# An attention and feed-forward kernel on one core: the last group's second layer as seven block products, and the first value loads on another queue

## The chip, the cores and the metric

The kernel runs on one core of a Trainium2 chip. A core has TensorE (PE in the profile, with PEld for its weight loads), VectorE (DVE), ScalarE (ACT), GpSimd (POOL) and SyncE (SP), each with its own instruction stream, which it works off in order; they wait for one another by semaphores only. DMAs are issued by SP or ACT and run on 16 DMA engines that all queues share. The metric is the device time of one execution, in microseconds; the figure for a kernel is the median of several runs.

## The reference

Two stages, for q, k, v of shape (4, 8, 768, 64) in float32:

```python
k_sum, v_sum = k.reshape(B, H, 24, 32, D).max(axis=3), v.reshape(B, H, 24, 32, D).mean(axis=3)
scores_l = where(|i - j| < 16, scale * q @ k.T, -1e9)
scores_s = scale * q @ k_sum.T + log(32)
a = softmax(concat([scores_l, scores_s], -1))
x = (a @ concat([v, v_sum])) -> (B, 768, 512)            # heads side by side
xn = (x - mean(x)) / sqrt(var(x) + 1e-6) * g_ln
out = x + maximum(xn @ w_ch1, 0) @ w_ch2                  # 512 -> 2048 -> 512
```

## The kernel before, in words

The 3072 rows are 24 tiles of 128 rows (T), and 12 groups of two tiles (g). Attention goes by half tiles (t = 0 to 47, four heads each). The first eight (t < 8, the `early_...` steps) work in float32 while the weights arrive; the others split every operand into a high and a low float16 part and sum three products (hh times high, hh times low, hl times high). The weights are fetched as 32 blocks (`fetch_w`, tile `raw`), decoded by DVE and ACT (`dec_w`, tile `wf`), scaled and split into two float16 parts (`conv_w`, tile `wp`).

The feed-forward layer of groups 0 to 5 is plain (`g1`, `g2`). Groups 6 to 11 (`SG = 6`) use seven block products in place of eight for the first layer (`split1`, `split2`, `sp1`; the sums of weight blocks are built by `combine`, tiles `wd`), and a plain second layer: `sp2`, two output tiles, each a sum of 8 times three products of 512 columns for either half q of the hidden units. For the very last tile and q = 1 that sum is cut into two halves of 256 columns (tile `last`). `kout` scales the result, a DVE instruction adds it to x (`scalar_tensor_tensor`, x<-a,wsc,x in the profile), and SP writes it out.

Steps only record their instructions. `Plan` then orders them: a list scheduler with a table of durations (`cost`, `ISSUE`, `LAND`, `RATE`), waits with some slack (`slack`), and random starts; the order that does best in a rehearsal with random DMA delays is issued. `LOADS` fixes the head of SP's queue (`in_front`), `BESIDE` says which of those loads ACT issues. Where the scheduler expects PE to stand idle before the weights are there, it fills in transposes (`spare`); `warm` puts 36 transposes at the start.

In the start, SP loads keys (k), queries (qw), the block matrix (blk), values (vw, two halves per tile) and weights; ACT issues the second half of the values of the first six tiles. PE works on score products (s), transposes of probabilities (pp), block means of values (v), outputs (o), transposes of normalised rows (tx) and then the first layer (h). In the profile nearly all instructions carry the line of the issuing helper, L437, so groups are told apart by tile names.

Of the kernel before, what the change touches and what calls it, by code (L numbers as in the profile page):

```python
# [50 lines left out]
SG = 6  # L51
# [11 lines left out]
LOADS = [("fetch_k0", 0), ("fetch_k0", 1), ("fetch_q", 0), ("gain",), ("fetch_blocks",), ("fetch_k0", 2), ("fetch_k0", 3)]  # L63
LOADS += [("fetch_v0", c) for c in range(7)] + [("fetch_tail", 0), ("fetch_q", 1), ("fetch_tail", 1), ("fetch_tail", 2)]
BESIDE = [("fetch_v0", c, 1) for c in range(6)]
# [33 lines left out]
def in_front(stage, engine):  # L99


    key = (stage[0], *stage[1][:1])
    return LOADS.index(key) if engine == "sync" and key in LOADS else None


class Plan:
# [6 lines left out]
    SETUP, TICK, SWITCH, FIRST = 1100, 10240 / 3, 93, 3500  # L113
    ISSUE = dict(transp=1550, lnT=1250, batch_vput=760, load_q=500)
    LAND = dict(fetch_v0=2050, fetch_k0=1950, fetch_q=2000, fetch_w=1750, fetch_tail=2000, gain=2000)
# [92 lines left out]
    def cost(self, engine, op, a, k, ins, outs):  # L208
# [3 lines left out]
        if op[:3] == "dma":  # L212
            x = (outs + ins)[0]
            return self.ISSUE.get(self.names[self.stage][0], 380 + 70 * (engine == "scalar")), x.ap[0][1] * free(x) * mybir.dt.size(x.dtype) / (200.0 if "transpose" in op else 360.0)
# [51 lines left out]
    def slack(self, x, y):  # L266

        name, a = self.names[x.stage]
        if x.engine == "tensor":
            if name in ("g1", "g2"):  # L270
                return SLACK2 * (a[0] >= 24)
            if name in ("sp1", "sp2"):
                return SLACK2 if name == "sp2" or self.names[y.stage][0] != "sp1" else SLACKP
            return SLACK * (name in ("qk", "pv", "batch_s"))
# [3 lines left out]
        late |= name in ("g1", "g2") and a[0] >= 24 or name in ("sp1", "sp2", "split1", "split2")  # L278
# [163 lines left out]
def body(ctx: ExitStack, tc, qt, qa, qe, kt, ks, va, vb, vs, g_ln, w1, w2, blocks, out):  # L442
# [654 lines left out]

    def operand(g, *names):
# [42 lines left out]
    def sp1(g, q):  # L1141
# [52 lines left out]
        keep("21", z)  # L1194
        product(x, "s4", plain(1, 1), last=True)
        keep("12", x)

# [32 lines left out]
    @pl.step  # L1230
    def gain():
        nc.sync.dma_start(gcol[:, 0], g_ln.rearrange("(c p) -> p c", p=P))
        nc.scalar.activation(gcol[:, 1], gcol[:, 0], AF.Copy, scale=SQ)

# [55 lines left out]

    warm()
# [37 lines left out]
    for t in range(8, 2 * TT + 1):  # L1329
# [82 lines left out]
```

## Time and profile before

| | |
|---|---|
| three runs | 615.63, 615.76, 616.48 us (median 615.76) |
| profiled execution | 614.82 us, of which span 613.0 us |
| mean granted TensorE clock | 0.997 (0.91 and 0.75 in the stretches 10 to 15 and 15 to 20 us) |
| HBM traffic | 66.27 MB read, 6.29 MB written |

The span runs from the first to the last instruction of the profiled execution; 1.8 us of its time lie around it. Busy shares are means over stages that have different limits, so the stretches in the rows below are cut where the stage changes: the first layer's first product starts at 48.46 us, the last matmul but six ends near 609.24 us. The duration of one matmul in the profile overlaps its neighbours; the pace of matmuls is read from the pieces of the chain of waits, where "x6" stands beside the time of six.

### The profile page before, as it was taken

How to read it: one execution, taken by the hardware profiler on the slowest of the kernel's cores; microseconds unless marked ns; L12 is line 12 of the kernel's file. 1: busy time of each engine (PE TensorE's matmuls, PEld its weight loads, DVE VectorE, ACT ScalarE, POOL GpSimd, SP SyncE). 2: the span in 40 equal slices, each digit the busy share in tenths (PEclk: the TensorE clock that was granted, in tenths of full speed). 3: DMA queues.
4: the chain of work that ended last, by engine and by line, in shares of the span. 5: the costliest groups of instructions: out<-in, count | busy, mean ns of one | idle time of the engine just before them, and what ended most of it. 6: DMA issues, size and time to landing. Idle time of an engine off the chain costs nothing.

```text
span 613.0 us, 15408 instructions
## 1 busy us (share of the span) xinstructions
PE 596.3 (97%) x5528; PEld 434.0 (71%) x5528; DVE 493.4 (80%) x1260; ACT 429.0 (70%) x1072; POOL 249.0 (41%) x473
## 2 busy tenths in 40 slices
PE   6998899999999999999999999999999999999997
PEld 5586777765677587776866876877777778766675
DVE  3899999999899899999798988889788974633232
ACT  3797798878999977799777857788686575331120
POOL 5122212124675575767664452645445333200000
PEclk9999999999999999999999999999999999999999
DMA  8991388636988977679966757569668461220000
GB/s 250 341 350 31 115 263 279 195 86 138 237 224 203 204 194 181 161 173 220 208 161 150 172 121 152 143 154 198 138 155 180 94 126 45 44 61 18 18 18 35
DMA packets 136237, 95.62 MB, mean 156 GB/s; under 512 B 94561, under 2 KB 118625, under 8 KB 136161
## 3 DMA queue, kind: packets, MB, share of 16 engines
q1 hardware_dynamic: 134528, 93.86, 60.6%
q8 instruction: 43, 0.70, 0.5%
q10 hardware_dynamic: 1632, 0.79, 0.5%
q14 instruction: 34, 0.27, 0.1%
HBM read 66.27 MB, written 6.29 MB: 118 GB/s over the span
## 4 chain that ended last, share of the span: by engine, by line
PE 75%; DVE 13%; DMA 5%; ACT 3%; POOL 2%; issue 1%; SPq 0%; ACTq 0%; POOLq 0%
PE a L437 34%; PE h L437 12%; PE qx L437 10%; PE qz L437 5%; PE s L437 4%; PE o L437 4%; PE qy L437 3%; DVE wf L437 2%; DMA vw<-in_va 1%; DVE raw L437 1%; DVE hl L437 1%; DVE wp L437 1%; PE v L437 1%; DMA ksg<-in_kt 1%; DVE p L437 1%
## 5 line engine op out<-in xcount | busy, mean ns | idle before, releaser
L437 PE MATMUL a<-wp,hh 128*128 128x512 f16 (+1 forms) x768 | 226.6, 377 | 0.0
L437 PEld LDWEIGHTS <-wp 128*128 128x128 f16 x2016 | 163.2, 98 | 25.0 <-issue 2.3
L437 PE MATMUL a<-wp,hl 128*128 128x512 f16 x384 | 144.8, 377 | 0.0
L437 PE MATMUL h<-xs,wp 128*128 128x256 f16 x1152 | 134.1, 273 | 2.2 <-DMA xs<-x 1.0
L437 PEld LDWEIGHTS <-hh 128*128 128x128 f16 x784 | 73.3, 98 | 65.3 <-issue 0.4
L437 POOL TENSOR_TENSOR p<-p,p 128x512 f16<-128x512 f32 x72 | 71.9, 1004 | 35.3 <-ACT p L437 24.5
L437 ACT ACTIVATE p<-p,mn,sv 128x184 f32<-128x184 f32 x144 | 76.1, 530 | 9.1 <-POOL mn L437 8.5
L437 PEld LDWEIGHTS <-hl 128*128 128x128 f16 x392 | 38.3, 98 | 44.6
L437 DVE SCALAR_TENSOR_TENSOR x<-a,wsc,x 128x512 f32<-128x512 f32 (+1 forms) x48 | 35.3, 736 | 22.4 <-PE a L437 22.1
L437 POOL COPY ksg<-ksum 128x48 f32<-128x48 f32 x72 | 29.3, 412 | 52.1 <-DMA ksg<-in_kt 44.8
L437 POOL TENSOR_TENSOR x<-x,rc 128x256 f32<-128x256 f32 x36 | 30.5, 847 | 42.5 <-DVE x L437 31.7
L437 POOL TENSOR_SCALAR mn<-mn,sv 128x2 f32<-128x2 f32 x72 | 31.1, 434 | 40.4 <-DVE mn L437 37.6
L437 DVE CUSTOM_DVE_ANT_0 p<-s,mask 128x184 f32<-128x184 f32 x144 | 42.7, 337 | 3.6 <-PE s L437 3.6
L437 PE MATMUL qx<-xs,wp 128*128 128x128 f16 x576 | 38.4, 219 | 0.0
L437 PEld LDWEIGHTS <-wd 128*128 128x128 f16 x576 | 33.8, 98 | 3.1
L437 DVE SCALAR_TENSOR_TENSOR kl<-ksg,sv,kh 128x368 f16<-128x368 f32 x48 | 34.2, 721 | 1.5 <-ACT kh L437 1.2
L437 ACT ACTIVATE kh<-ksg,sv 128x368 f16<-128x368 f32 x48 | 28.5, 594 | 9.4 <-PE s L437 3.4
L437 DVE SCALAR_TENSOR_TENSOR hl<-h,hh 128x512 f16<-128x512 f32 x48 | 32.3, 678 | 2.0 <-ACT hh L437 1.8
L437 ACT CAST p<-p 128x512 f16<-128x512 f32 x72 | 33.3, 505 | 0.2
L437 ACT ACTIVATE v<-vst,sv 128x512 f16<-128x512 f32 x36 | 25.7, 716 | 9.2 <-PE o L437 7.8
L437 DVE SCALAR_TENSOR_TENSOR v<-vst,sv,v 128x512 f16<-128x512 f32 x36 | 30.2, 838 | 1.3 <-ACT v L437 1.1
L437 ACT ACTIVATE hh<-h 128x512 f16<-128x512 f32 x48 | 28.0, 584 | 4.4 <-PE h L437 4.3
(209 smaller groups left out, 1217.0 us busy)
## 6 DMA issues: line engine op xcount, KB each, us to landing
raw<-in_w SPq DMA_DIRECT2D x32, 512.0 KB
ksg<-in_kt SPq DMA_DIRECT2D x72, 184.0 KB
out_x<-x SPq DMA_DIRECT2D x23, 256.0 KB
qw<-in_qt SPq DMA_DIRECT2D x36, 128.0 KB
vst<-in_va SPq DMA_DIRECT2D x36, 128.0 KB
qs<-in_qt SPq DMA_DIRECT2D x36, 128.0 KB
vst<-in_vb SPq DMA_DIRECT2D x80, 32.0 KB
bst<-in_ks SPq DMA_DIRECT2D x12, 192.0 KB
```

The lines of the kernel that those rows point to most:

```text
L437: getattr(getattr(nc, self.ops[i].engine), op)(*a, **k)
```

## The change

Three things are edited. The group g = 11 (`SH = 11`) gets a second layer of seven block products of 256 columns (`sq2`): `sp1` then also builds sums of the rectified hidden blocks (s1 to s4), and `combine2` builds sums of blocks of the second weight matrix (tiles y, we) on POOL, DVE and ACT, in the places of tiles that attention no longer needs (`WE`). The six value halves move from ACT's queue to SP's (`BESIDE = []`), and a step `table` puts a dummy exponential at the head of ACT. The planner's table of the first loads' durations is changed and `LOADS` is reordered.

```diff
-SG = 6
+SG, SH = 6, 11
...
-BESIDE = [("fetch_v0", c, 1) for c in range(6)]
+LOADS += [("fetch_v0", c) for c in range(7)] + [("fetch_tail", 0), ("fetch_w", 0), ("fetch_q", 1), ("fetch_tail", 1)]
+LOADS += [("fetch_w", 1), ("fetch_tail", 2)]
+BESIDE = []
...
-    SETUP, TICK, SWITCH, FIRST = 1100, 10240 / 3, 93, 3500
+    SETUP, TICK, SWITCH, FIRST = 1100, 10240 / 3, 93, 1300
...
+    def combine2(k, u):
+        top, low = (wt[2, 4 * k + 2 * i + u] for i in range(2))
+        if (k, u) == (0, 0):
+            late["y"] = [work("x", f"y2_{i}", [P, DM], F32, XB) for i in range(2)]
+        y = late["y"]
+        for x, w in zip(y, (top, low)):
+            nc.gpsimd.tensor_tensor(x[:], w[:, 0], w[:, 1], ALU.add)
+        l, r = slice(0, 256), slice(256, DM)
+        yt, yb = y
+        nc.vector.tensor_tensor(yb[:, r], yb[:, r], yt[:, r], ALU.subtract)
+        nc.vector.tensor_tensor(yt[:, r], yt[:, r], yt[:, l], ALU.subtract)
+        nc.vector.scalar_tensor_tensor(yt[:, l], yt[:, l], -1.0, yb[:, r], ALU.mult, ALU.subtract)
+        nc.vector.tensor_tensor(yb[:, l], yb[:, l], yt[:, l], ALU.add)
+        n = 4 * k + 2 * u
+        both = [work(WE[n + i], f"we{n + i}", [P, 2, DM], F16) for i in range(2)]
+        for x, d in zip(y, both):
+            nc.scalar.copy(d[:, 0], x[:])
+            nc.vector.tensor_tensor(d[:, 1], x[:], d[:, 0], ALU.subtract)
+        tt[2, k, u] = both
...
-        keep("21", z)
+        if g < SH:
+            keep("21", z)
+            product(x, "s4", plain(1, 1), last=True)
+            keep("12", x)
+            return
+        b = [work(n, f"{n}_s{g}_{q}_{i}", [P, 4, P], F32, 2) for n in ("xn", "x16") for i in range(2)]
+        def both(name, x):
+            hh = work("hh", f"hh{name}{g}_{q}", [P, 4, P], F16, HB)
+            hl = work("hl", f"hl{name}{g}_{q}", [P, 4, P], F16, HB)
+            nc.scalar.copy(hh[:], x[:])
+            nc.vector.tensor_tensor(hl[:], x[:], hh[:], ALU.subtract)
+            quad[g, q, name] = hh, hl
+        stt = nc.vector.scalar_tensor_tensor
+        nc.scalar.activation(b[0][:], z[:], AF.Relu)
+        stt(b[1][:], seven[:], 0.0, b[0][:], ALU.max, ALU.add)
+        stt(b[0][:], y[:], 0.0, b[0][:], ALU.max, ALU.subtract)
+        stt(b[2][:], y[:], 0.0, b[1][:], ALU.max, ALU.subtract)
+        both("s2", b[2])
+        both("s3", b[0])
+        both("s1", b[1])
         product(x, "s4", plain(1, 1), last=True)
         keep("12", x)
+        stt(b[3][:], x[:], 0.0, b[2][:], ALU.max, ALU.add)
+        both("s4", b[3])
...
+    def sq2(g, q):
+        def product(ps, x, w, first=False, last=False):
+            hh, hl = quad[g, q, x]
+            for u in range(4):
+                if u % 2 == 0:
+                    pl.joined = None
+                for n, (h, a) in enumerate(((hh, 0), (hh, 1), (hl, 0))):
+                    nc.tensor.matmul(
+                        ps, h[:, u], w(u, a), start=(first and u == 0 and n == 0),
+                        stop=(last and u == 3 and n == 2), skip_group_check=True,
+                    )
+                if u % 2:
+                    pl.joined = False
+        def plain(i, j):
+            return lambda u, a: wt[2, 4 * (2 * q + u // 2) + 2 * i + u % 2][:, a, 256 * j : 256 * j + 256]
+        def made(i, j):
+            return lambda u, a: tt[2, 2 * q + u // 2, u % 2][i][:, a, 256 * j : 256 * j + 256]
+        def add(ps, i, j):
+            x = xt[2 * g + i][:, 256 * j : 256 * j + 256]
+            nc.vector.scalar_tensor_tensor(x, ps, kout[:, q : q + 1], x, ALU.mult, ALU.add)
+        def done(i, j):
+            if q == 1:
+                T, cs = 2 * g + i, slice(256 * j, 256 * j + 256)
+                nc.sync.dma_start(out[T * P : T * P + P, cs], xt[T][:, cs])
+        x, y, z = (psum(n, f"r{n}{g}_{q}", [P, DM])[:, :256] for n in "sas")
+        product(x, "11", plain(0, 0), True)
+        add(x, 0, 0)
+        product(x, "s2", made(0, 0))
+        add(x, 1, 0)
+        product(z, "s3", made(1, 1), True)
+        add(z, 1, 1)
+        product(x, "s1", made(0, 1))
+        add(x, 1, 1)
+        done(1, 1)
+        product(z, "22", made(1, 0), last=True)
+        add(z, 1, 0)
+        done(1, 0)
+        product(y, "12", plain(1, 0), True, True)
+        add(y, 0, 0)
+        done(0, 0)
+        product(x, "s4", plain(1, 1), last=True)
+        add(x, 0, 1)
+        done(0, 1)
...
+    def table():
+        nc.vector.memset(wacc[:, :1], 0.0)
+        nc.scalar.activation(wacc[:, :1], wacc[:, :1], AF.Exp)
...
-        while done < NG and t >= 4 * done + 4:
+        while done < NG and t >= (4 * done + 4 if done < SH else 2 * TT):
+            if done == SH:
+                for n in range(8):
+                    combine2(n // 2, n % 2)
...
-                    sp2(done, q)
+                    (sp2 if done < SH else sq2)(done, q)
```

The order of the instructions is planned anew, so it changes everywhere. Three places follow. The first is the head of ACT's queue; vw are values, k keys, kx their copies for the score products, p probabilities. Before:

```order
L437 DMA vw_100<-in_va 128x2x128
L437 DMA vw_101<-in_va 128x2x128
L437 DMA vw_102<-in_va 128x2x128
L437 DMA vw_103<-in_va 128x2x128
L437 DMA vw_104<-in_va 128x2x128
L437 DMA vw_105<-in_va 128x2x128
L437 ACT_TABLE_LOAD
L437 COPY kx<-k_0_90 128x158
L437 COPY kx<-k_1_91 128x128
```

and in the change:

```order
L443 ACT_TABLE_LOAD
L443 ACTIVATE wacc<-wacc 128x1
L443 COPY kx<-k_0_90 128x158
L443 COPY kx<-k_1_91 128x128
L443 COPY kx<-k_2_92 128x158
L443 COPY kx<-k_3_93 128x128
```

The six loads in front of the table load are gone, and the copies stand third. The second place is SP's queue from the third key load to the first weight load (raw). Before:

```order
L437 DMA k_2_92<-in_ks 128x768
L437 DMA k_3_93<-in_ks 128x768
L437 DMA vw_100<-in_va 128x2x128
L437 DMA vw_101<-in_va 128x2x128
L437 DMA vw_102<-in_va 128x2x128
L437 DMA vw_103<-in_va 128x2x128
L437 DMA vw_104<-in_va 128x2x128
L437 DMA vw_105<-in_va 128x2x128
L437 DMA vend<-in_vb 32x2x256
L437 DMA qw_95<-in_qe 128x512
L437 DMA raw_254<-in_w 128x1024
```

and in the change:

```order
L443 DMA k_2_92<-in_ks 128x768
L443 DMA k_3_93<-in_ks 128x768
L443 DMA gcol<-in_g_ln 128x4x1
L443 DMA vw_100<-in_va 128x2x128 x2
L443 DMA vw_101<-in_va 128x2x128 x2
L443 DMA vw_102<-in_va 128x2x128 x2
L443 DMA vw_103<-in_va 128x2x128 x2
L443 DMA vw_104<-in_va 128x2x128 x2
L443 DMA vw_105<-in_va 128x2x128 x2
L443 DMA vend<-in_vb 32x2x256
L443 DMA vst_77<-in_vb 32x2x128 x2
L443 DMA raw_253<-in_w 128x1024
```

Six value loads, the gain (gcol, formerly fourth in the queue) and two small loads (vst) now stand ahead of the first weight load, and the second query load (qw_95) behind it. The third place is the end of DVE's queue; hl and hls are low parts of hidden blocks, x_s and xn_s their sums, we low parts of the new weight sums, y their staging, x the output. Before, its last instructions are:

```order
L437 TENSOR_TENSOR qz_1_1495<-qz_1_1495,two_1_1499 128x512
L437 SCALAR_TENSOR_TENSOR hl_1_1502<-seven_1_1500,hh_1_1501 128x512
L437 SCALAR_TENSOR_TENSOR x_1454<-a_0_1_1492,wsc,x_1454 128x512
L437 SCALAR_TENSOR_TENSOR hl_1_1504<-qz_1_1495,hh_1_1503 128x512
L437 SCALAR_TENSOR_TENSOR hl_1_1506<-qx_1_1493,hh_1_1505 128x512
L437 SCALAR_TENSOR_TENSOR x_1416<-a_1_0_1507,wsc,x_1416 128x512
L437 SCALAR_TENSOR_TENSOR x_1454<-a_1_1_1508,wsc,x_1454 128x256
L437 SCALAR_TENSOR_TENSOR x_1454<-last,wsc,x_1454 128x256
```

and in the change the stretch from the sum that ends q = 0 on begins with:

```order
L443 SCALAR_TENSOR_TENSOR x_1416<-rs_0_1519,wsc,x_1416 128x256
L443 TENSOR_TENSOR seven_1_1529<-qx_1_1522,seven_1_1529 128x512
L443 SCALAR_TENSOR_TENSOR y_0_1477<-y_0_1477,y_1_1478 128x256
L443 SCALAR_TENSOR_TENSOR xn_s_1_1_1533<-seven_1_1529,xn_s_1_0_1532 128x512
L443 TENSOR_TENSOR y_1_1478<-y_1_1478,y_0_1477 128x256
L443 SCALAR_TENSOR_TENSOR x_s_1_0_1534<-qy_1_1523,xn_s_1_1_1533 128x512
L443 SCALAR_TENSOR_TENSOR x_1416<-ra_0_1520,wsc,x_1416 128x256
L443 TENSOR_TENSOR we_1493<-y_0_1477,we_1493 128x512
L443 SCALAR_TENSOR_TENSOR xn_s_1_0_1532<-qy_1_1523,xn_s_1_0_1532 128x512
L443 SCALAR_TENSOR_TENSOR x_1416<-rs_1_1546,wsc,x_1416 128x256
L443 TENSOR_TENSOR hls_1_1537<-x_s_1_0_1534,hhs_1_1536 128x512
```

Here 25 instructions stand from that sum to the end: 10 adds into x (256 columns), 2 of y (256) and 13 of 512. The 8 rows of before cover a longer stretch of PE's work.

## Rows read from the trace of the kernel before

**Rows 1.** Busy time by stretch: span of the stretch, then its length and for each engine the busy microseconds (and instructions), TensorE's granted clock, the DMA share and GB/s.

```profile
0.00:20.00 20.00, 14.85 (x73) 10.97 (x75) 7.21 (x28) 7.33 (x20) 8.60 (x53) 0.91 0.91 274
20.00:48.46 28.46, 26.19 (x203) 21.19 (x202) 27.14 (x92) 25.07 (x70) 6.67 (x19) 1.00 0.91 319
48.46:100.00 51.54, 47.72 (x372) 36.04 (x370) 50.39 (x136) 45.83 (x124) 11.56 (x28) 1.00 0.53 172
100.00:200.00 100.00, 98.66 (x745) 69.19 (x743) 93.38 (x238) 85.69 (x225) 43.53 (x74) 1.00 0.69 182
200.00:500.00 300.00, 298.98 (x3032) 220.87 (x3031) 268.94 (x679) 234.56 (x574) 166.33 (x277) 1.00 0.73 165
500.00:609.24 109.24, 109.24 (x1112) 75.45 (x1110) 45.34 (x89) 30.48 (x63) 12.28 (x23) 1.00 0.17 37
```

**Rows 2.** The chain of waits that ended last, its pieces near the end: start, length, engine and tile, number of instructions.

```profile
595.50 1.34 PE qz L437 x24
596.84 1.29 PE a L437 x6
...
602.72 1.97 PE last L437 x18
604.69 4.55 PE a L437 x30
609.24 0.67 PE last L437 x6
...
609.93 0.48 DVE x L437
```

**Rows 3.** The timeline of the first 20 us, on all engines: start, length, engine, operation, count, and in brackets the idle time before it with what ended it (SPq and ACTq are DMA issues).

```profile
0.72 0.87 SPq L437 DMA_DIRECT2D k<-in_ks  x2
...
0.89 7.25 ACTq L437 DMA_DIRECT2D vw<-in_va  x6
...
1.59 6.89 PE L437 MATMUL warm<-ident 128*128 128x128 f32 x36 [1.59 <-POOL ident masks.py:199]
...
2.32 0.62 SPq L437 DMA_DIRECT2D gcol<-in_g_ln  x1
...
3.90 0.34 SPq L437 DMA_DIRECT2D blk<-in_blocks  x1
...
3.91 0.95 DVE L437 TENSOR_REDUCE kmax<-k 128x24 f32<-128x768 f32 x1 [2.91 <-DMA k<-in_ks]
...
5.65 1.98 SPq L437 DMA_DIRECT2D k<-in_ks  x2
...
8.03 3.94 SPq L437 DMA_DIRECT2D vw<-in_va  x6
...
8.22 1.28 ACT L437 ACT_TABLE_LOAD   x1 [8.22 <-DMA vw<-in_va]
...
9.52 0.52 ACT L437 COPY kx<-k 128x158 f32<-128x158 f32 x2
...
9.94 0.91 PE L437 MATMUL s<-kx,qw 64*128 64x184 f32 x8 [1.35 <-issue]
...
11.01 0.36 DVE L437 CUSTOM_DVE_ANT_0 p<-s,emask 128x192 f32<-128x192 f32 x1 [4.40 <-PE s L437]
...
13.12 0.91 SPq L437 DMA_DIRECT2D raw<-in_w  x2
...
14.00 1.85 PE L437 MATMUL v<-vw,blk 128*120 128x512 f32 x2
...
17.78 0.36 DVE L437 CUSTOM_DVE_ANT_0 p<-s,emask 128x192 f32<-128x192 f32 x1 [3.86 <-PE s L437]
...
18.88 0.42 DVE L437 TENSOR_SCALAR wf<-raw 128x512 uint32<-128x512 uint32 x1
```

**Rows 4.** The timeline around the first product of the first layer, PE and DVE.

```profile
42.67 4.09 PE L434 MATMUL spare<-ident 128*128 128x128 f32 x36
...
47.97 0.66 PE L437 MATMUL tx<-ident,xn 128*128 128x128 f32 x4 [1.20 <-DVE xn L437]
...
48.46 2.79 PE L437 MATMUL h<-xs,wp 128*128 128x256 f16 x24
```

**Rows 5.** The instructions on the tiles room, yt and wd, that is `combine` for the first layer's weight sums: duration in ns as least, median and greatest, first and last start, form.

```profile
L437 DVE TENSOR_TENSOR room<-room,yt x16: 384/408/1356, 151.7 to 334.3; 128x256 f32<-128x256 f32 x16
L437 POOL TENSOR_TENSOR yt<-wp x8: 1148/1152/1523, 131.4 to 323.9; 128x512 f32<-128x512 f16 x8
L437 DVE TENSOR_TENSOR wd<-yt,wd x4: 672/690/926, 165.9 to 280.7; 128x512 f16<-128x512 f32 x4
L437 ACT CAST wd<-yt x4: 607/612/613, 165.2 to 272.4; 128x512 f16<-128x512 f32 x4
```

**Rows 6.** DVE's timeline in a stretch of the late first layer where four instructions of 512 columns follow each other.

```profile
581.07 0.70 DVE L437 TENSOR_TENSOR qz<-qz,two 128x512 f32<-128x512 f32 x1 [7.14 <-PE qz L437]
581.68 0.68 DVE L437 SCALAR_TENSOR_TENSOR hl<-qx,hh 128x512 f16<-128x512 f32 x1
582.36 0.75 DVE L437 SCALAR_TENSOR_TENSOR x<-a,wsc,x 128x512 f32<-128x512 f32 x1
583.03 0.68 DVE L437 SCALAR_TENSOR_TENSOR hl<-qz,hh 128x512 f16<-128x512 f32 x1
```

**Rows 7.** Who waited for whom from 500 us on: waiting engine and tile, what ended the wait, microseconds in total, number, longest.

```profile
DVE x L437 <- PE a L437: 21.7, 11, 6.4
```

More of the change, by code (lines that the diff above doesn't have):

```diff
@@ L62 @@
 FILL_IN, FILL_END = 500, 800
-LOADS = [("fetch_k0", 0), ("fetch_k0", 1), ("fetch_q", 0), ("gain",), ("fetch_blocks",), ("fetch_k0", 2), ("fetch_k0", 3)]
-LOADS += [("fetch_v0", c) for c in range(7)] + [("fetch_tail", 0), ("fetch_q", 1), ("fetch_tail", 1), ("fetch_tail", 2)]
-BESIDE = [("fetch_v0", c, 1) for c in range(6)]
+LOADS = [("fetch_k0", 0), ("fetch_k0", 1), ("fetch_q", 0), ("fetch_blocks",), ("fetch_k0", 2), ("fetch_k0", 3), ("gain",)]
+LOADS += [("fetch_v0", c) for c in range(7)] + [("fetch_tail", 0), ("fetch_w", 0), ("fetch_q", 1), ("fetch_tail", 1)]
+LOADS += [("fetch_w", 1), ("fetch_tail", 2)]
+BESIDE = []
 NV = 3
@@ L99, in in_front @@
 def in_front(stage, engine):
+    if stage[0] == "table":
+        return 0
     key = (stage[0], *stage[1][:1])
@@ L112 @@
     SAME = dict(tensor=0, vector=127, scalar=143, gpsimd=100, sync=0)
-    SETUP, TICK, SWITCH, FIRST = 1100, 10240 / 3, 93, 3500
-    ISSUE = dict(transp=1550, lnT=1250, batch_vput=760, load_q=500)
-    LAND = dict(fetch_v0=2050, fetch_k0=1950, fetch_q=2000, fetch_w=1750, fetch_tail=2000, gain=2000)
+    SETUP, TICK, SWITCH, FIRST = 1100, 10240 / 3, 93, 1300
+    ISSUE = dict(transp=1550, lnT=1250, split1=1250, split2=1250, batch_vput=760, load_q=500)
+    ISSUE |= dict(fetch_v0=650, fetch_tail=430, fetch_q=420, fetch_k0=430, gain=430)
+    RATE = dict(fetch_v0=300.0, fetch_w=410.0, fetch_q=385.0)
+    LAND = dict(fetch_v0=2050, fetch_k0=1950, fetch_q=2000, fetch_w=1550, fetch_tail=2000, gain=3000)
     LAND |= dict(batch_q=1350, batch_v=1300, load_q=1350, load_v=1150, transp=1050)
@@ L213, in cost @@
             x = (outs + ins)[0]
-            return self.ISSUE.get(self.names[self.stage][0], 380 + 70 * (engine == "scalar")), x.ap[0][1] * free(x) * mybir.dt.size(x.dtype) / (200.0 if "transpose" in op else 360.0)
+            return self.ISSUE.get(self.names[self.stage][0], 380 + 70 * (engine == "scalar")), x.ap[0][1] * free(x) * mybir.dt.size(x.dtype) / (200.0 if "transpose" in op else self.RATE.get(self.names[self.stage][0], 360.0))
         if engine == "tensor":
@@ L277, in slack @@
         late |= name in ("ln", "lnT") and a[0] >= LATE // 2
-        late |= name in ("g1", "g2") and a[0] >= 24 or name in ("sp1", "sp2", "split1", "split2")
+        late |= name in ("g1", "g2") and a[0] >= 24 or name in ("sp1", "sp2", "sq2", "split1", "split2")
         if not late:
@@ new lines, in sp1 @@
+        both("s4", b[3])
+    @pl.step
+    def sq2(g, q):
[41 more added lines that the diff above has]
+        done(0, 1)
@@ L1289, in batch @@
         batch_s(b)
+    table()
     warm()
```

5 lines of the change are left out of this document (4 added, 1 removed).

## The prediction, made before the change was run

> **What bounds the kernel now.** I read the busy time by stretch first, because the shares of the whole span mix stages. The reader is to see there [rows 1] that TensorE sets the end: from 200 us on it is busy 298.98 of 300.00 and then 109.24 of 109.24 us at a granted clock of 1.00, the upper of its two levels (2.4 GHz). DVE is the bound before: 27.14 of 28.46 us busy from 20 us to the first layer's first product, and 50.39 of the next 51.54. In the first 20 us nobody is full; DVE is busy for 7.21. From 500 us on DVE is busy for 45.34 of 109.24 us and POOL for 12.28, so there 63.9 us of DVE lie idle.
>
> Second, the pieces of the chain that ended last, for the pace of matmuls [rows 2]: six of 512 columns in 1.29 us (0.215 each), eighteen of 256 columns in 1.97 us (0.109 each), 24 of 128 columns in 1.34 us (0.056 each). Nothing but PE stands there until the last add of 0.48 us.
>
> Third, the timeline of the first 20 us [rows 3], for what DVE waits for. ACT issues value loads from 0.89 to 8.14 us, then loads its table until 9.50, then makes the key copies; the first score product follows at 9.94, though PE's warm-up transposes end at 8.48, and the first softmax instruction of DVE at 11.01 after 4.40 us of waiting. The second softmax waits 3.86 us more and starts at 17.78, and only behind it, at 18.88, comes the first weight decode.
>
> **The change, part by part.** Sums are made against the profiled execution's 614.82 us. The median of the runs is 615.76, so 0.94 is added at the end.
>
> *PE's work in the last group.* Before, the second layer of group 11 is 24 matmuls for a tile and a half q: 72 of 512 columns, and 48 of 256 for the last tile. At the paces of [rows 2] this is 72 x 0.215 = 15.48 and 48 x 0.1094 = 5.25, together 20.73 us. After, it is 7 products x 12 matmuls x 2 halves = 168 of 256 columns, 18.38 us. That takes away 2.35 us, on the path, since PE has no idle time there.
>
> The row shows that width is paid in full: 512 columns cost 1.96 times as much as 256 [rows 2]. The Trainium skill ("TensorE: Matmul & The Clock Gate", "Wait — 56ns, not 53.3ns?") gives 2.5 ns for each matmul besides its columns; going by that, the 48 more matmuls would cost about 0.1 us of the saving, and the paces of the rows hold that cost already.
>
> *Work for the other engines.* DVE gets from `combine2` 32 instructions of 256 columns and 16 of 512: by the medians on room and wd [rows 5] 32 x 0.408 + 16 x 0.69 = 24.1 us. The sums of hidden blocks and their low parts are 14 more of 512 columns at 0.68 [rows 6], 9.5 us. The adds into x become 14 of 256 columns at 0.48 [rows 2] in place of three of 512 at 0.75 [rows 6] and two of 256, some 3.6 us. Together 37 us, into 63.9 us of idle time [rows 1]. POOL gets 16 additions of 1.15 us and ACT 16 copies of 0.61 [rows 5] and some for the hidden blocks, both into mostly idle engines. I cost all this at nothing as long as it is done before the last stretch; the cover is PE's 109 us.
>
> *The last stretch.* This is where the cover ends. In the new order 25 instructions of DVE stand from the sum that ends q = 0 to the end. In that time PE has 36 matmuls of 128 columns (2.0 us) and, for the second layer of q = 1 and what is left of q = 0, 108 of 256 (11.8 us), 13.8 us in all. DVE has 13 of 512 columns, which follow each other every 0.65 us (from 581.07 to 583.03 in three steps [rows 6]), 8.5 us; 12 of 256 at 0.41 to 0.42 when they overlap likewise (0.408 in [rows 5]), 5.0 us: 13.5 us. So DVE, which now waits 21.7 us for PE's second-layer sums in eleven waits [rows 7], will have no room here, and a product that needs a hidden sum can wait for it. In the other direction, an add into x that waits for its product holds up the hidden sums queued behind it on DVE, and these PE waits for. The lower bound is 0: every sum is there in time. The upper is 4.6 us: the 13 instructions of 512 stand end to end with PE waiting for them (8.5 us), less the 36 matmuls (3.9 us) of the three products (11, 22, 12) whose hidden blocks are plain and need none of these sums. I take 0.8, nearer the lower, because seven of the 13 read first-layer results of which all but the last are ready when the stretch begins. The end itself stays one add of 256 columns and one output transfer.
>
> What speaks against this is contention. The 256-column subtractions on room took 384 to 1356 ns with a median of 408, and POOL's additions on yt 1148 to 1523 [rows 5]: some instructions were lengthened by up to 0.95 us. The Trainium skill ("SBUF — State Buffer", "Who interferes with whom") says that a DVE instruction with two SBUF inputs contends with a GpSimd instruction that reads SBUF, over a port that one of them holds at a time. By that rule `combine2`, which puts both kinds side by side, would be slowed, and the spread in the rows agrees in sign; the first rival below has its own price from the rows.
>
> *The start.* SP issues the six value halves, at 3.94/6 = 0.66 us each [rows 3] some 3.9 us more, and two small loads more and one query load less ahead of the first weight load: 4.3 us. On the other side SP now stands idle between issues, from 2.94 to 3.90, from 4.24 to 5.65 and inside the 1.98 us that two key loads take (0.87 at the very start), together 3.5 us [rows 3]; I take these to be waits for room in flight that ACT's loads took. If they all go, the first weight load is issued at 13.12 + 4.3 - 3.5 = 13.9 us, if none, at 17.4; I take 14.3. Queued behind it are all other weight loads and the second query load. ACT is free at some 2.5 us in place of 9.5, so the first score product can start when the warm-up ends, 8.5 us, a gain of at most 1.4 us for it. The first softmax then comes between 9.6 us and no gain, 11.3, if the keys' last load, whose maximum now stands ahead of it in DVE's queue (0.95 us each), is as late as now. PE's next scores stand behind products of the first two value tiles (1.85 us for two [rows 3]); the second softmax comes at 12.5 to 16.5 us in place of 17.78. So both are done when the first weights land, and the first decode waits for the weights alone: 17.3 to 21.3 us; I take 17.9 against 18.88. In DVE's queue some 2.6 us less stand between the first decode and the first product of the first layer, by the rows before it in the two orders. What DVE gains here lasts, since it bounds the time until about 100 us, and PE's last wait before that product is one for DVE, 1.20 us [rows 4]. I take 1.5 us of gain in all, bounds 5 us of gain (no idle time is left on SP and all of the earlier softmax and the 2.6 us count) and 1.5 us of loss (the weights come late by 4, less 2.6). The 21 more filling transposes at 4.09/36 = 0.114 us [rows 4], 2.4 us of PE, stand in PE's wait for the weights; with that wait gone they would cost up to that, which the lower gain holds.
>
> *The rest of the new order.* From 48 to 500 us PE is idle for 3.82 + 1.34 + 1.02 = 6.2 us [rows 1]; a new order can win or lose part of it. I take 0, with 1.5 to either side.
>
> Sum: 614.82 - 2.35 + 0.8 - 1.5 = 611.8; with 0.94, 612.7 us.
>
> **The rivals.** *The end goes to DVE (slower).* POOL's 16 additions and DVE's subtractions hold each other up, each by up to 0.95 us [rows 5], some 15 us in all; as the staging tiles exist once, the whole chain of POOL, DVE and ACT (about 1.15 x 2 + 4 x 0.41 + 2 x 0.69 = 5.3 us for each of eight blocks, 43 us) runs late into the last stretch and DVE is the bound there. For it: 13.5 of 13.8 us, and the last additions of y stand in that stretch. Against it: 63.9 us of idle time ahead, and a median that hardly differs from the least. It decides when more than three such pairs (3 us, what the forecast gains) fall into the last stretch; with six of the sixteen there, 5.7 us, the time is 612.7 + 5.7 = 618.4 us. Chance 0.10.
>
> *The start gains nothing.* DMA engines are busy for 0.91 of the first 48 us [rows 1]; if bytes and not the order of issue set when weights come, the earlier softmax only lengthens a wait. Against it: DVE, not a DMA, is what PE waits for at the first product [rows 4]. 612.7 + 1.5 = 614.2 us. Chance 0.15.
>
> *SP's longer queue delays the weights.* None of SP's waits goes, and the first decode comes 1.6 us later than now after the 2.6 us of saved work have been counted only in part: 615.8 us. For it: nothing in the rows proves that SP's waits are ACT's doing. Chance 0.08.
>
> *The start gains twice.* All of SP's waits go, and DVE has room besides: 4.9 us in place of 1.5, 609.3 us. For it: 12.8 us of idle DVE in the first 20. Chance 0.10.
>
> **How the numbers follow.** The forecast, 612.7 us, with the bounds of its own small terms (611 to 614) has 0.57. The range takes in the early case at the lower end, with 0.3 below it for its own spread, and at the upper all but the slowest rival, with 0.7 above the delayed weights: 609.0 to 616.5. A measurement of this kernel can tell some 0.2%, 1.2 us, from no change: faster means below 614.5. That holds for the forecast, the early case and half of the case without gain at the start: 0.75. Same: the other half and the delayed weights, 0.15. Slower, above 617, holds only for a bad end or a worse new order: 0.10.
>
> **What the changed profile would show.** The start is right if ACT's table load begins before 2 us, the first scores stand at about 8.6, the second softmax before 16.5, the first decode at 17.3 to 18.5 and the first product of the first layer at 45, plus or minus 2 (now 48.46). PE's work is right if twelve matmuls of 256 columns take 1.31 us in the last group. The end is right if DVE is nearly without idle time in the last 14 us and PE's waits there add up to 0.8, at most 2. I am wrong if PE waits for hidden sums by more than that, if the first decode comes after 19, or if PE's idle time from 48 to 500 us is more than 1.5 us away from 6.2.

## The result, and the profile after

| | before | after |
|---|---|---|
| median of 11 runs each, one chip | 615.76 us (614.25 to 617.17) | 619.75 us (616.18 to 621.00) |
| profiled execution, its span | 614.82, 613.0 us | 618.53, 616.5 us |
| mean granted clock in it | 0.997 | 0.992 |

The ratio is 1.006, interval 1.0042 to 1.0079: slower by some 3.7 us (0.006 x 615.8), where 3.05 us of gain were forecast. The forecast of 612.7 us and its range to 616.5 both missed. Three executions of the experiments below, one each of `e1_layer_only`, `e2_start_only` and `e3_key_first`, took 878.7, 884.6 and 3525.1 us and are left out of the ratios.

First the view that is read first, busy time by stretch, here of the changed kernel in the columns of [rows 1]:

```profile
0.00:20.00 20.00, 17.21 (x91) 11.88 (x93) 8.15 (x30) 9.50 (x26) 8.62 (x53) 1.00 0.84 255
20.00:48.46 28.46, 25.80 (x227) 23.06 (x223) 25.94 (x91) 22.66 (x65) 7.58 (x19) 1.00 0.89 332
48.46:100.00 51.54, 46.03 (x325) 36.05 (x323) 47.68 (x124) 42.86 (x114) 6.94 (x22) 0.90 0.46 147
100.00:200.00 100.00, 97.26 (x737) 68.64 (x735) 93.26 (x246) 87.37 (x232) 42.52 (x77) 1.00 0.72 193
200.00:500.00 300.00, 299.36 (x2933) 217.28 (x2932) 264.39 (x669) 230.50 (x567) 166.97 (x276) 1.00 0.72 162
500.00:609.24 109.24, 109.21 (x1264) 84.09 (x1262) 85.81 (x170) 49.67 (x98) 36.66 (x43) 1.00 0.21 46
609.24:616.50 7.26, 4.07 (x38) 3.40 (x35) 3.04 (x7) 0.35 (x1) 0.00 (x0) 1.00 0.21 72
```

Set beside [rows 1], the last 109 us look as forecast: DVE has 40.5 us more work there (85.81 against 45.34; some 37 were forecast), POOL 24.4, and PE is still busy throughout. The third row is the one to stop at. PE issues 325 matmuls where it issued 372, its idle time is 5.51 in place of 3.82 us, and its clock is 0.90 in place of 1.00: 0.10 x 51.54 = 5.2 us of full speed lost. Before, 0.09 x 20 = 1.8 us were lost, in the first 20 us. From 48 to 500 us PE is idle for 5.51 + 2.74 + 0.64 = 8.9 us, where it was 6.2. DVE, the bound until 100 us, has 3.86 us of idle time in that third row against 1.15 before.

The same columns at 5 us each, from 50 to 80 us, show where in that stretch:

```profile
50.00:55.00 5.00, 3.86 (x29) 2.78 (x26) 5.00 (x17) 3.47 (x11) 1.20 (x3) 1.00 0.01 3
55.00:60.00 5.00, 4.29 (x23) 3.39 (x22) 4.08 (x16) 3.76 (x11) 1.04 (x4) 0.68 0.00 0
60.00:65.00 5.00, 4.97 (x30) 4.48 (x30) 4.43 (x12) 4.89 (x12) 0.00 (x0) 0.64 0.09 26
65.00:70.00 5.00, 5.00 (x48) 4.36 (x45) 3.79 (x11) 3.92 (x17) 0.74 (x2) 1.00 0.83 235
70.00:75.00 5.00, 1.55 (x11) 1.34 (x9) 4.30 (x8) 2.87 (x8) 0.25 (x2) 0.88 0.33 109
75.00:80.00 5.00, 5.00 (x37) 4.35 (x36) 4.99 (x18) 3.01 (x9) 1.40 (x4) 0.77 0.30 84
```

The clock falls twice from its upper level (2.4 GHz) to its lower one (1.2 GHz), each time behind idle time of PE: 1.14 us in 50 to 55, and 3.45 us in 70 to 75. The timeline below shows the same two output matmuls (o) before and after the clock's return: 0.80 us, then 0.44. The DMA column shows another thing: almost no transfer from 50 to 65 us, then 235 GB/s.

The timeline of that stretch, with the idle time before an instruction and what ended it in brackets:

```profile
54.33 0.78 PE L443 MATMUL pp<-ident,p 128*128 128x128 f32 x3 [1.12 <-ACT p L443]
...
62.76 0.80 PE L443 MATMUL o<-vst,pT 128*128 128x130 f32 x2
...
63.87 0.44 PE L443 MATMUL o<-vst,pT 128*128 128x130 f32 x2
...
66.05 0.36 SPq L443 DMA_DIRECT2D bst<-in_ks  x1
...
70.70 0.55 DVE L443 TENSOR_REDUCE kmax<-bst 128x12 f32<-128x384 f32 x1 [1.92 <-DMA bst<-in_ks]
...
73.66 0.94 PE L443 MATMUL tx<-ident,xn 128*128 128x128 f32 x4 [3.44 <-DVE xn L443]
```

and SP's longest wait between 36 and 80 us, in the table of waits (total, number, longest):

```profile
SPq L443 <- PE o L443: 14.2, 1, 14.2
```

SP stands for 14.2 us, until 59.93, behind one load whose place PE has to free, and 3.9 us more behind a weight load whose place DVE has to free. The keys of the next batch (tile bst) are queued behind both, are issued at 66.05 and land 4.65 us later, and DVE, then PE wait for them. Whether SP's waits are what holds the keys is tested by `e3_key_first`. In the kernel before, DVE waits for no load between 36 and 80 us.

The start, as in [rows 3]:

```profile
0.72 1.28 ACT L443 ACT_TABLE_LOAD   x1 [0.72 <-PEq L1514]
...
4.02 8.27 SPq L443 DMA_DIRECT2D vw<-in_va  x12
...
7.75 0.91 PE L443 MATMUL s<-kx,qw 64*128 64x184 f32 x8
...
12.76 0.36 DVE L443 CUSTOM_DVE_ANT_0 p<-s,emask 128x192 f32<-128x192 f32 x1 [2.28 <-PE s L443]
...
13.93 0.42 SPq L443 DMA_DIRECT2D raw<-in_w  x1
...
15.82 0.42 SPq L443 DMA_DIRECT2D raw<-in_w  x1
...
17.80 0.43 DVE L443 TENSOR_SCALAR wf<-raw 128x512 uint32<-128x512 uint32 x1 [3.85 <-DMA raw<-in_w]
...
21.41 0.43 DVE L443 TENSOR_SCALAR wf<-raw 128x512 uint32<-128x512 uint32 x1 [1.73 <-DMA raw<-in_w]
...
44.06 0.38 PE L443 MATMUL h<-xs,wp 128*128 128x256 f16 x2
```

The marks set for the start are met: the table load before 2 us, the second softmax at 12.76, the first decode at 17.80, the first product of the first layer at 44.06. The first scores, at 7.75, come 0.85 us before their mark. Yet DVE's idle time up to 48.46 us is 11.85 + 2.52 = 14.37 us against 12.79 + 1.32 = 14.11 before: on the engine that bounds this part nothing was gained.

The end of the chain of waits, as in [rows 2]:

```profile
588.07 1.31 PE rs L443 x12
...
605.24 1.53 PE rs L443 x14
606.77 0.03 issue
606.80 1.27 PE rs L443 x10
608.07 1.31 PE ra L443 x12
609.38 3.94 PE rs L443 x36
613.32 0.03 issue
613.35 0.48 DVE x L443
```

Twelve matmuls of 256 columns take 1.31 us, as forecast, and in the last stretch PE waits for nobody.

### The profile page after: what moved, and what is told of

Read it like the earlier page. It is cut to its first block, busy times and chain, and to the rows that moved or that the text cites. A ratio compares the mean times of both kernels' runs of the same rounds, so it can differ in the third digit from the quotient of the medians.

```text
span 616.5 us, 15679 instructions
## 1 busy us (share of the span) xinstructions
PE 598.9 (97%) x5597; PEld 444.4 (72%) x5597; DVE 528.3 (86%) x1332; ACT 442.9 (72%) x1097; POOL 269.3 (44%) x489
## 4 chain that ended last, share of the span: by engine, by line
PE 77%; DMA 9%; DVE 8%; ACT 3%; issue 1%; SPq 1%; POOL 0%; ACTq 0%; POOLq 0%; DVEq 0%
PE a L443 33%; PE h L443 15%; PE qx L443 10%; PE qz L443 5%; PE s L443 4%; DMA raw<-in_w 4%; PE o L443 4%; PE rs L443 3%; PE qy L443 3%; DMA bst<-in_vs 2%; DVE wf L443 2%; DVE raw L443 1%; SPq L443 1%; DVE p L443 1%; DMA k<-in_ks 1%
## 5 line engine op out<-in xcount | busy, mean ns | idle before, releaser
L443 PE MATMUL a<-wp,hh 128*128 128x512 f16 x704 | 209.4, 379 | 0.0
L443 PE MATMUL a<-wp,hl 128*128 128x512 f16 x352 | 133.4, 379 | 0.0
L443 PEld LDWEIGHTS <-hh 128*128 128x128 f16 x752 | 70.7, 98 | 61.1 <-issue 0.5
L443 POOL TENSOR_TENSOR p<-p,p 128x512 f16<-128x512 f32 x72 | 75.9, 1060 | 20.7 <-ACT p L443 14.5
L443 PEld LDWEIGHTS <-hl 128*128 128x128 f16 x376 | 36.8, 98 | 41.8
L443 POOL TENSOR_SCALAR mn<-mn,sv 128x2 f32<-128x2 f32 x72 | 33.3, 465 | 49.8 <-DVE mn L443 49.5
L443 POOL COPY ksg<-ksum 128x48 f32<-128x48 f32 x72 | 25.0, 351 | 55.4 <-DMA ksg<-in_kt 52.0
L443 DVE SCALAR_TENSOR_TENSOR x<-a,wsc,x 128x512 f32<-128x512 f32 x44 | 32.5, 740 | 14.4 <-PE a L443 14.3
L443 POOL TENSOR_TENSOR y<-wp 128x512 f32<-128x512 f16 x16 | 20.1, 1262 | 27.0 <-DVE we L443 27.0
```

What stands on the lines that cost most here:

```text
L443: getattr(getattr(nc, self.ops[i].engine), op)(*a, **k)
```

## The experiments

Three explanations stood against each other; the recorded expectations call them theories. Theory A: the new start and what is planned behind it cost the time, by late loads, by DVE's waits for them (DVE being the bound until about 100 us) and by the clock, which falls behind PE's waits between 50 and 75 us. Theory B: the work that the layer adds for DVE and POOL costs it. Theory C: the draw, that is, every new plan differs from the old one by some microseconds whatever the edit. Ratios are to the kernel before on the same chip, with 95% intervals. The experiments ran on four chips, so a difference between two ratios carries the error of both.

**Either part alone, planned anew.** `e1_layer_only` has the new layer with the old loads, table of durations and ACT queue; `e2_start_only` has the new start with the old layer.

```diff
 # e1_layer_only, from the changed kernel
...
-LOADS += [("fetch_v0", c) for c in range(7)] + [("fetch_tail", 0), ("fetch_w", 0), ("fetch_q", 1), ("fetch_tail", 1)]
...
-BESIDE = []
...
+LOADS += [("fetch_v0", c) for c in range(7)] + [("fetch_tail", 0), ("fetch_q", 1), ("fetch_tail", 1), ("fetch_tail", 2)]
+BESIDE = [("fetch_v0", c, 1) for c in range(6)]
...
-    SETUP, TICK, SWITCH, FIRST = 1100, 10240 / 3, 93, 1300
...
+    SETUP, TICK, SWITCH, FIRST = 1100, 10240 / 3, 93, 3500
...
-    table()
...
 # e2_start_only, from the changed kernel
-SG, SH = 6, 11
+SG, SH = 6, 12
```

> The seven block products alone, with the loads, their queues and the planner's table of before. If the loss comes from the new start and what is planned behind it (theory A), this keeps the 2.35 us of TensorE's work and runs at 612 to 615 us against 615.8 before, with TensorE free of waits in the last 14 us. If the added work of DVE and POOL is what costs (theory B), it is slower than before, 618 or more, and the waits stand after 500 us. If any new plan of this size is worse than the one of before by chance (theory C), it is within 2 us of 615.8 with waits somewhere between 48 and 250 us.

> The new loads, the early table load and the planner's new table alone; the last group's second layer stays as before. Theory A: the first product of the first layer comes near 44 us as in the changed kernel, but DVE waits for key and value blocks between 60 and 130 us by some 5 us in all, TensorE's granted clock falls in one or two stretches, and the time is 2.35 us above the changed kernel's, 621 to 622. Theory B: 615.8 less the gain at the start, 611 to 613. Theory C: anything from 612 to 622, with waits at other places than in the changed kernel.

Measured: 1.0028 (0.9994 to 1.0062) for the layer, 1.0085 (1.0045 to 1.0125) for the start. The layer alone is within the 2 us that theory C allows, and above theory A's 612 to 615 us; the start alone is where theory A put it. So the loss is there without the layer: it comes with the start or with its plan. By the middle values the layer takes 1.0085 - 1.006, some 1.5 us, off it, but the two intervals leave 1.2 us the other way as well. In the profile of `e2_start_only` PE waits 2.56 us for tx at 73.25 us, and the clock falls in the same two places.

`e5_layer_again` is the kernel of `e1_layer_only` once more, for its profile.

> The kernel of the first experiment once more, for a profile. If the layer's own work cost the time (theory B), the waits of TensorE stand after 500 us. If the new plan does (theory C), TensorE's work after 300 us is as far ahead as the 2.35 us that the layer saves, less 1, and the lost time stands between 48 and 250 us.

One execution took 619.16 us. Its table of waits shows what the old loads do in a new plan:

```profile
DVE wf L440 <- DMA raw<-in_w: 5.5, 3, 4.0
```

DVE's idle time to 48.46 us is 16.2 us there, 2.1 more than before, with no edit to the start at all: the plan alone moved it. PE is idle for 3.92 + 3.33 + 1.69 = 8.9 us from 48 to 500 us, and for 0.13 in the 109 us behind them; the clock stays at 1.00 from 20 to 609 us. So the waits stand where theory C puts them and not where theory B does, and a new plan can lose by idle time alone, without the clock.

**The waits and the clock.** `e3_key_first` moves the late key load ahead of a weight load and two small value loads on SP; `e4_fill` puts 40 transposes that nobody reads (0.114 us each, [rows 4]) where PE waits between 50 and 75 us; `e7_before_fill` does the like to the kernel before, with 36.

```diff
 # e3_key_first, at the end of the planning, from the changed kernel
...
+        key, old = find("sync", ("batch_k", (1, 1)), "dma_start"), find("sync", ("load_v", (12,)), "dma_start")
+        key = min(key, key=best[1].__getitem__)
+        for n, i in enumerate(find("sync", ("fetch_w", (17,)), "dma_start") + sorted(old, key=best[1].__getitem__)[1:]):
+            best[1][i] = best[1][key] + 1 + n
 # e4_fill, from the changed kernel
...
+        for e, name, count in (("early_transp", (6, 0), 9), ("early_transp", (6, 1), 2), ("early_pv", (6, 0), 4), ("lnT", (3,), 25)):
+            at = min(best[1][i] for i, x in enumerate(self.ops) if x.engine == "tensor" and self.names[x.stage] == (e, name))
+            fills = fills + [at - 1] * count
```

> The changed kernel with one key load (the second block of keys of batch 1) moved in SP's queue ahead of one weight load and two small value loads that wait for other engines; nothing else differs. Theory A: the key load is issued at 62 in place of 66.05 us, DVE's wait of 1.92 us for it and with it TensorE's wait of 3.44 us go, and the clock's fall at 74 us, which follows that wait, goes too: 3.4 + 1.7 = 5 us faster than the changed kernel, 614 to 616. If the time is lost elsewhere (theory B, or the first fall of the clock at 57 us), no more than 1 us is gained.

> The changed kernel with 40 more of the filling transposes on TensorE, 15 before the early transposes and outputs of the fourth tile (53 to 56 us), where it waits for ACT, and 25 before the transpose that waits 3.44 us for DVE at 70 us; no other instruction moves. [...]

> The kernel before with 36 more filling transposes in the places where its own trace shows TensorE waiting between 46 and 72 us. If a falling clock costs the kernel before as well in part of its runs (its granted clock is between 0.989 and 0.997 there), the clock stays at 0.997 and the time falls by 1 to 2 us, to 614 to 615.5; then the fill's gain in the changed kernel is partly one that both kernels could have. If the clock of before falls only at its start, nothing is gained, or up to 1 us lost to the fill.

`e3_key_first`: 1.0026 (1.0002 to 1.0049), less than expected. Its timeline at the same place:

```profile
66.04 0.35 SPq L448 DMA_DIRECT2D bst<-in_ks  x1
...
69.83 0.52 DVE L448 TENSOR_REDUCE kmax<-bst 128x12 f32<-128x384 f32 x1
...
72.76 0.63 PE L448 MATMUL tx<-ident,xn 128*128 128x128 f32 x4 [1.41 <-DVE xn L448]
```

The keys are issued no earlier, since SP then waits for ACT to free their tile, so SP's waits in front of them were not what held them; but they land earlier. PE waits 1.41 us in place of 3.44, and the second fall of the clock is gone (1.00 from 70 to 80 us). The first stays (0.62 from 55 to 60).

`e4_fill`: 0.9999 (0.9979 to 1.002), with a median of 616.31 us. I had forecast 615 to 616.5 if the falls follow from the waits, and 619 to 620 or more if they don't. The stretch reads:

```profile
48.46:100.00 51.54, 49.38 (x389) 38.85 (x387) 50.34 (x135) 45.21 (x122) 9.50 (x26) 1.00 0.51 168
```

The clock is 1.00, 389 matmuls (40 of them the fills) are issued in place of 325, and DVE is busy for 50.34 us in place of 47.68. Some 4.6 us of work that serves for nothing made the kernel 0.0061 x 615.8 = 3.75 us faster (2.0 to 5.5 by the two intervals). The mean clock of its ten runs is 1.000 in nine and 0.999 in one; runs of the changed kernel at 0.997 took 616.2 to 617.4 us, those at 0.989 to 0.992 took 618.5 to 621.0. `e7_before_fill`: 0.9991 (0.9973 to 1.0009). In its profile, as in that of the kernel before, the clock is 1.00 from 20 to 609 us; where it doesn't fall in that stretch, fills bring nothing that can be told from none.

**The order held.** `e9_layer_old_order`, `e10_start_old_order` and `e11_both_old_order` carry the layer, the start, and both. The start is here the six value loads on SP and the table load at ACT's head; the planner's new durations and the reordered `LOADS` are left out, so the second query load stays ahead of the first weight load. A list of numbers gives the order that the kernel before has for all that was planned in its first 480 us, and each engine works off that list before the scheduler chooses freely.

```diff
...
-            if not left[i]:
+            if not left[i] and (back or i not in self.held):
...
+                if lines[e]:
+                    if not left[lines[e][-1]]:
+                        can.append((max(free[e], ready[lines[e][-1]], 1000.0), k))
...
+            if lines[e]:
+                i = lines[e].pop()
...
+        self.lines = {e: [i for i in self.head(e) if self.ops[i].engine == e] for e in self.ENGINES}
 # e10 and e11, on the kernel before's loads
-BESIDE = [("fetch_v0", c, 1) for c in range(6)]
+BESIDE = []
...
```

> The seven block products alone, and every instruction that the kernel before plans in its first 480 us held in exactly that kernel's order on every engine; only the rest is planned anew. If the new order is what costs (theories A and C), TensorE's saving of 2.35 us comes out nearly whole: 0.2 to 0.4% below the kernel before, about 613.5 where that runs at 615.8. If the added work itself costs (theory B), it is at or above the time of before.

> The start alone on the order of before: the six value loads move from ACT's queue to SP's, the table load goes to the head of ACT, the gain's load stands behind the keys; all other instructions keep the order of before (nine filling transposes in place of seven at 70 us). If DVE bounds the time until about 100 us and its idle time at 48 us is what counts (theory A), the time falls by as much as DVE's idle time at 48 us falls below the 14.1 us of before: I expect 0 to 1 us. If an earlier first score product is worth its 1.4 us, it gains 1.4 or more. If SP's longer queue delays the weights, it loses 1 to 2.

> The seven block products and the start's edits together on the order of before (the first 480 us). By theory A the sum of the two runs beside it: 2.35 us of the layer and 0 to 1 of the start below before, 612.5 to 613.5 where before runs at 615.8, so below both kernels; the difference to the changed kernel, some 6 us, is then the price of the new order and of the clock that falls in it.

Measured on one chip: layer 0.9997 (0.9972 to 1.0021), start 0.9995 (0.9976 to 1.0015), both 0.9976 (0.9952 to 1.0000), 614.79 us. The layer and the start, which cost 3.7 us with a new plan, gain some 1.5 us in the old order, and `e11_both_old_order` has the lowest ratio of all, though its interval ends at 1.0000; 612.5 to 613.5 us were expected of it. `e9_layer_old_order` lies between what theories A and C and what theory B let expect, and doesn't decide by itself. How much of the difference between the two plans comes from the reordered `LOADS` and the new durations, and how much from the draw, these runs don't tell. Of `e9_layer_old_order`, the stretch in which PE had 1.02 us of idle time in [rows 1], and the chain at its end:

```profile
200.00:500.00 300.00, 300.00 (x2971) 218.54 (x2970) 263.17 (x666) 228.88 (x556) 160.88 (x271) 1.00 0.73 164
```

```profile
602.33 0.61 DVE hl L506
...
602.98 1.27 PE ra L506 x10
604.25 3.94 PE rs L506 x36
608.22 0.48 DVE x L506
```

In this order the chain does pass through DVE's hidden sums before 602.98, and PE is idle for some 0.7 us in the last stretch: the forecast's 0.8 fits this plan, though not that of the changed kernel. Of `e10_start_old_order`, by stretch:

```profile
0.00:20.00 20.00, 16.15 (x81) 11.65 (x81) 8.12 (x31) 7.76 (x22) 9.33 (x56) 1.00 0.90 271
20.00:48.46 28.46, 25.45 (x195) 21.85 (x194) 26.62 (x91) 25.18 (x71) 6.82 (x16) 0.94 0.90 321
```

DVE's idle time is 11.88 + 1.84 = 13.72 us against 14.11, a gain of 0.4. The time, 0.3 us lower, agrees with that, but can't be told from no gain either. The same stretch of `e11_both_old_order`:

```profile
20.00:48.46 28.46, 26.82 (x186) 23.41 (x186) 24.75 (x88) 24.73 (x69) 5.69 (x15) 0.82 0.91 319
```

DVE's idle time is 11.85 + 3.71 = 15.56 us there, 1.45 more than before, behind a clock of 0.82. So the old order doesn't keep the clock from falling, and in this execution the start lost time on DVE.

**Other draws.** `e8_second_plan` takes the order that came second in the changed kernel's rehearsal, with the fills; `e13_before_second` and `e14_before_third` take the second and third of the kernel before, without any edit.

```diff
 # e8_second_plan and e13_before_second; e14_before_third has [2]
...
-        return found[self.scores.index(min(self.scores))]
+        return found[self.scores.index(sorted(self.scores)[1])]
...
```

> The changed kernel in another of the orders that its planner kept, the one that came second in its rehearsal, with the same rule for the filling transposes at the same four places. If the loss lies in the particular order (theory C), the time differs by 2 us or more from the 616.3 of the first order with the fill, either way, and DVE's waits stand at other loads. If it lies in the change itself, it is within 1 us of 616.3.

> The kernel before, unchanged but for its order: the order that came second in its planner's rehearsal is issued in place of the first. If the changed kernel lost by its edits to loads and planner's table, this is within 1 us of the kernel before (615.8). If the order of before was one good draw among many, so that any new plan loses (theory C), this is slower by 2 to 6 us, as the changed kernel (4.0), the layer alone with a new plan (1.5 to 2.5), the start alone with a new plan (6.3 at 622.2) and the changed kernel's second order (4.3) were.

> The same with the order that came third in the rehearsal. By theory C slower than before by 2 to 6 us; by the other theory within 1 us of it. If one of the two orders is within 1 us and the other is not, the draw matters, but new plans are not worse as a rule.

Measured: 1.0054 (1.0024 to 1.0084), 1.0008 (0.9984 to 1.0032), 1.0047 (1.0027 to 1.0068). A kernel with nothing changed but the draw can lose 2.9 us, or nothing, and the changed kernel's second order is some 3.4 us slower than its first with the same fills. In the profile of `e14_before_third`, an execution of 622.23 us (its median is 620.08), the loss is for the most part plain idle time of PE, 3.16 + 3.56 us from 100 to 500 us in place of 1.34 + 1.02 [rows 1], with a clock of 0.98 in the first of the two rows:

```profile
100.00:200.00 100.00, 96.84 (x715) 67.65 (x714) 91.57 (x237) 84.73 (x220) 41.86 (x71) 0.98 0.71 186
200.00:500.00 300.00, 296.44 (x2969) 217.74 (x2967) 260.01 (x655) 228.08 (x559) 158.63 (x270) 1.00 0.71 163
```

That every new draw is worse isn't shown: `e13_before_second` is equal. Nor is it shown whether the planner's changed table of durations made bad draws likelier.

**Who bounds.** `e6_weight_first` is `e4_fill` with the second weight load directly behind the first on SP; `e12_dve_work` gives DVE of the kernel before 16 needless reductions ahead of the first layer's start there.

```diff
 # e6_weight_first
...
+        best[1][one] = best[1][zero] + 0.5
 # e12_dve_work
...
+            if i == stop:
+                for _ in range(16):
+                    nc.vector.tensor_reduce(self.tab[:], self.ones[:], axis=AX.X, op=ALU.max)
...
```

> The changed kernel with the 40 filling transposes, and the second weight load moved in SP's queue ahead of a query load and two small value loads, directly behind the first. If DVE's 1.73 us of waiting for that load at 21 us is what ate the gain of the start (theory A, since DVE bounds the time until about 100 us), DVE's idle time at 30 us falls from 13.3 to about 12 and the time is 1.0 to 1.5 us below that of the fill alone, some 615. If DVE is not the bound there, the time stays at that of the fill alone, 616.3.

> The kernel before with 16 reductions of 128 columns, whose result nobody reads, put into DVE's queue in front of the low part of the first hidden block (about 52 us). If DVE is the bound until about 100 us (theory A), their whole time, some 3 us, is added to the time of the kernel. If TensorE or transfers bound it there, 1 us or less is added.

`e6_weight_first`: 1.0011 (0.9991 to 1.0032). DVE's idle time to 30 us falls from 13.3 to 12.7 us, half as far as expected, and to 48.46 us it is 13.76. The time doesn't follow within what can be told: not confirmed. But the fills no longer hold the clock in every execution: five of the ten are at 0.994 to 0.997, in the profiled one with 0.97 from 48 to 100 us, and take 616.8 to 618.7 us; the five at 0.999 or more take 614.6 to 617.0. So this run doesn't decide. `e12_dve_work`: 1.0106 (1.0075 to 1.0137), 6.5 us. The group of reductions, PE's wait behind it, and the stretch:

```profile
L439 DVE TENSOR_REDUCE tab<-ones x16: 280/286/286, 51.6 to 56.4; 128x1 f32<-128x128 f32 x16
```

```profile
57.35 0.59 PE L441 MATMUL wps<-wacc,ones 128*128 128x4 f32 x2 [4.61 <-DVE hl L441]
```

```profile
48.46:100.00 51.54, 44.32 (x329) 33.61 (x328) 49.02 (x135) 39.99 (x109) 9.26 (x24) 0.93 0.44 140
```

The reductions hold DVE for 5.1 us (I had reckoned with some 3), and the kernel loses 4.6 to 8.4 us, where 1 or less was expected if DVE isn't the bound there: it is. Not all of the 6.5 us need be DVE's own: behind PE's longer wait the clock is 0.93 in a stretch where it was 1.00, 3.6 us of full speed, and the two prices aren't told apart.

## Why the prediction was wrong, and where it was right

**The step that failed** is "*The rest of the new order.* From 48 to 500 us PE is idle for 3.82 + 1.34 + 1.02 = 6.2 us [rows 1]; a new order can win or lose part of it. I take 0, with 1.5 to either side." Both edits in the old order gave 0.9976, planned anew 1.006: the new order costs 0.84%, 5.2 us. The two intervals together leave it between some 3.3 and 7 us, but not 1.5. It was sized by idle time alone, as if an order could lose no more than a part of what was idle already, and the prediction has no term for a clock that falls. Of the 5.2 us, fills in PE's waits bring back 3.75 (2.0 to 5.5): that part is the clock, behind waits of 1.1 to 3.4 us. The remaining 1.5 us is not taken apart further. The 5.2 us hold the reordered `LOADS` and the planner's new durations as well as the draw. The sign given at the end of the prediction was met: PE's idle time from 48 to 500 us is 8.9 us, 2.7 away from 6.2. The chance of slower, 0.10, named "a worse new order" without a price; other draws of the unchanged kernel would have given one, though a low one (none and 2.9 us in the two that were run).

**The start: marks right, worth wrong.** The first weight load was issued at 13.93 (14.3 forecast), so SP's idle time did go with ACT's loads; first decode and first product came as forecast. But I added "what DVE gains here lasts" to PE's dates. DVE's idle time fell by 0.4 us in the old order and rose by 0.3 in the new, since the second weights came behind a query load and two small loads and DVE waited 1.73 us for them at 21.41. The term was 1.5. The start alone measured 0.3 us and, as the difference between both edits and the layer, 1.3; within the spread of the runs these don't differ, nor from none. The profile of `e11_both_old_order`, with 1.45 us more idle time on DVE than before, speaks against the 1.3. Of the rivals on the start, that it gains nothing is nearest in its number; its reason, that bytes set when the weights come, isn't tested: the first decode did come earlier (17.80 against 18.88), but from 20 to 45 us the DMA engines' share is 0.97 to 1.03 in the kernel before and 0.90 to 1.03 in the changed one.

**PE's work in the last group: right in the pace, not confirmed in full.** 18.38 us for 168 matmuls needs 0.1094 each; the rows give 1.31 us for twelve. With the last stretch's 0.8 against it, the forecast nets 1.55 us; the two pairs that differ by the layer with the order held (`e9_layer_old_order` and the kernel before, `e11_both_old_order` and `e10_start_old_order`) give 0.2 and 1.2 us, and the changed kernel against `e2_start_only`, each with its own plan, 1.5. None of the three is clear of noise, and where the rest of the 2.35 us stays isn't settled.

**The last stretch: right about DVE, too high for this plan.** DVE runs without a gap from 598.8 to 611.3 us, as forecast, but PE doesn't wait: 0.06 us of issue in place of 0.8. In the plan of `e9_layer_old_order` the 0.8 fits, so that it depends on the plan too.

**The rival of the slower end is false.** The groups of `combine2` in the changed kernel (least, median and greatest in ns, first and last start):

```profile
L443 POOL TENSOR_TENSOR y<-wp x16: 1146/1154/2074, 528.9 to 597.1; 128x512 f32<-128x512 f16 x16
L443 DVE TENSOR_TENSOR y<-y,y x16: 385/419/426, 540.7 to 601.5; 128x256 f32<-128x256 f32 x16
L443 DVE TENSOR_TENSOR we<-y,we x16: 679/684/1634, 545.1 to 605.5; 128x512 f16<-128x512 f32 x16
```

Single instructions were lengthened, by up to 0.95 us as in [rows 5], but the medians are those of before. The rule of the Trainium skill ("SBUF — State Buffer", "Who interferes with whom") therefore has no weight here: the trace agrees with it for single instructions at most. The chain of eight blocks did run late, over 77 us (528.9 to 605.5) and not 43, as POOL waits 27.0 us for its two staging tiles; PE needed the sums no sooner.

Taken together: 3.05 us of gain were forecast. Some 1.5 (between 0 and 3.0) are there when the order is held, and 5.2 us are lost to the new order, which gives 3.7 us slower.

## What to carry to other kernels

Where an edit makes a planner draw a new order, give the draw its own term, with a price measured on the unchanged kernel (here 0 to 2.9 us without an edit, and 5.2 us with this one); or hold the old order, which tells the edit from the draw. Where an engine other than PE bounds a stretch, count that engine's idle time and not the dates at which PE's products come: here the first product of the first layer came 4.4 us earlier and DVE gained nothing. A wait of PE of one or a few microseconds can cost again through the clock, and work that serves for nothing, put into the wait, is a cheap cover, but only where the profile shows that the clock falls.

## What was not expected of the hardware

Waits of PE of 1.1 and 3.4 us were followed by stretches in which the granted clock was 0.64 to 0.88, 5.2 us of full speed in all; what decides it stays open, since the kernel before has as much idle time from 55 to 60 us and keeps 1.00 (its row, in the columns of the 5 us above):

```profile
55.00:60.00 5.00, 3.85 (x33) 3.09 (x31) 4.90 (x19) 5.00 (x12) 1.86 (x4) 1.00 0.05 16
```

Executions of the changed kernel differ with it: 616.2 us at a mean clock of 0.997, 621.0 at 0.991. Taking six loads off ACT's queue gave SP's issues some 3.5 us: the first weight load was issued 13.93 - 13.12 = 0.8 us later in place of 4.3. And a key load issued behind a weight load and two small value loads, with one more weight load right behind it, landed 4.65 us after its issue (66.05 to 70.70), with the DMA engines busy for 0.83 of the time from 65 to 70 us; with those loads behind it, in `e3_key_first`, it was there after 3.8 us at most.
